# Longer wo runs and, in the last pass of a decode kernel's backward, held stores, a later dQ and an earlier ask for weight slabs

## The chip, the cores and the metric

The kernel runs on one core of one Trainium2 chip. The metric is device time of the whole program in microseconds (us), as the median of a kernel's runs. The kernel before took 2029.06 us (median of 3 runs, 2028.84 to 2034.46). Kernels are compared by their ratios to the kernel before.

"Half clock" below means stretches where the profile shows TensorE's granted clock at 0.50. The records of the clock hold 0.5 and 1.0 only; a 0.8 in a table is a mean over a stretch.

## The reference

Two layers of attention over a cache and of a feed-forward block with squared ReLU, for one token, then the gradients of everything by `jax.vjp`. Biases, reshapes and the set-up of inputs are cut.

```python
# D=1024, 32 query heads, 4 kv heads, 65536 cached positions, head size 128, F=3584, bf16
def attn(x, k_cache, v_cache, wq, wo):
    q = (x @ wq).reshape(1, 1, 32, 128).transpose(0, 2, 1, 3)
    k = jnp.repeat(k_cache, 8, axis=1); v = jnp.repeat(v_cache, 8, axis=1)
    p = softmax(jnp.einsum("bhqd,bhkd->bhqk", q, k) * 128 ** -0.5)
    o = jnp.einsum("bhqk,bhkd->bhqd", p, v)
    return o.transpose(0, 2, 1, 3).reshape(1, 1, 4096) @ wo
def ffn(x, w1, b1, w2, b2):
    h = x @ w1 + b1
    r = jnp.where(h > 0, h, 0)
    return (r * r) @ w2 + b2
x = x + attn(layernorm(x), k_cache, v_cache, wq, wo); x = x + ffn(layernorm(x), ...)
x = x + attn(layernorm(x), k_cache, v_cache, wq, wo); x = x + ffn(layernorm(x), ...)   # same weights
# outputs: x, and the gradients of x, k_cache, v_cache, wq, wo, w1, b1, w2, b2
```

Both layers use the same caches and weights, so dK and dV (67 MB each) are sums over two layers and are written once. The same holds for the weight gradients, which are sums of two outer products.

## The kernel before

The caches are read once for the forward of each layer and once or twice in the backward: four attention passes. The last pass reads V and K and writes dV and dK. In it, background work (the weight gradients, and products with the rows of wo and wq for the gradient that runs back through the layer) is taken up between the items of the pipeline. An item is 8 blocks of 128 positions of one kv head; the pass has 256 items, 64 per head ("group").

All big transfers use an arena of 1 MB places: 12, and eight more while the pass runs on, as the planes that hold the saved scores are given back group by group. SP (SyncE) issues the loads in order, POOL (GpSimd) the stores in order. A place whose store was just issued counts as five steps younger, and in the last pass a load takes the youngest place that has been free for nine steps.

```python
    def take_one(fill, load=False):
        by_age = sorted((t, i) for i, t in FREE.items())
        if load and PS["pass4"]:
            early = [i for t, i in by_age if t <= NOW["step"] - AHEAD]       # AHEAD = 9
            i = early[-1] if early else by_age[0][1]
            ...
    class Slot:
        def free(self, stored=False):
            for k in range(self.n):
                give_slot(self.i + k, STORE_STEPS if stored else 0)          # STORE_STEPS = 5

    def wo_slabs(g, ahead=1):                       # rows of 2 KB, one per partition and k
        v = rows_of(A_wo)
        return slabs("s_wo", lambda k, kn: v[:, g * R + k:g * R + k + kn, :], R, 4, 1024, ahead, True)

    def g_rowdots(slab_it, nk, vcol, nj, finish, name):
        ...
        for kc, slab in slab_it:
            if vbc is None:
                vbc = yield from g_bcast_vec(vcol, nj)
            elif kc % 4 == 0:
                for _ in range(WAIT_STEPS):         # 5 items between one slab and the next
                    yield "wait"
            t = mvs.tile([P, n], BF, name="mv_t", tag="mv_t", bufs=2)
            nc.vector.tensor_tensor(out=t[:, :], in0=slab, in1=vbc[:, :], op=ALU.mult)
            ...

        def by_group(self, p, gen):
            ...
                self.later.append((k * n + n // 2 if PS["pass4"] else k * n + n // 4, gen(g), g))
```

The last pass itself. `ps_gg` is the PSUM tile in which dV, dK and the weight gradients arrive; `evac` copies it to the arena on ACT (ScalarE) or DVE (VectorE), whichever has less planned work.

```python
        def outer16(name, out, key, xt, gg, j1):           # 16 blocks of dV or dK
            if j1 == 0:
                state[key] = Slot(name, True)
            stg = state[key].t[:, :].rearrange("p (j d) -> p j d", d=DH)
            for m in range(2):
                pg = ps_gg()
                for h in range(2):
                    nc.tensor.matmul(pg[:, 512 * h:512 * h + 512], lhsT=xt[64 * h:64 * h + 64, j1 // 8 + m, :],
                                     rhs=gg[64 * h:64 * h + 64, :, :].rearrange("p a b -> p (a b)"), ...)
                evac(stg[:, jj:jj + 8, :].rearrange("p j d -> p (j d)"), pg[:, :], kind="f32")
            if j1 + 16 == J:                               # J = 32
                nc.gpsimd.dma_start(out=out, in_=stg)      # 1 MB
                state.pop(key).free(stored=True)

        def k8(g, c8):                                     # dQ, and dK
            kb8 = kv8("k", g, c8)
            ...
            for i in range(8):
                nc.tensor.matmul(ps_dq[:, 0:w, :]..., lhsT=kb8[:, i, :], rhs=X[:, s:s + w, :]..., ...)
            ...
                if glast[g] // SU == su:
                    on_group(g)
            if 2 * j0 >= J:
                outer16("gstk", half(GKv, g, b), "stk", xt, state[("GG", g, su)][0], 2 * j0 - J)

        pipeline(items, [(vT, 0), (vS, TLEAD), (dV8, DV_LAG), (k8, B4_LAG)], bg, end)   # lags 0, 2, 3, 7

    def rank2(out, lhs, rhs):                              # weight gradients: 2 rows, one per layer
        n = out.shape[1]
        pg = ps_gg()
        for h in range(n // 512):
            r = slice(64 * h, 64 * h + 2)
            nc.tensor.matmul(pg[:, 512 * h:512 * h + 512], lhsT=lhs(r), rhs=rhs(r), ...)
        evac(out, pg[:, 0:n], kind="f32")

    def on4(g):                                            # when dQ of a group is complete
        if g != lastg[3]:
            bg.add(g_dn(L1, dn1, g, g == firstg[3]))       # product with the wq slabs
            bg.normal.append(gwq(g))
        else:
            PRE["rows"].run()
            ...
    attn_bwd4(3, L1, L3, on4, bg, b4, [(12 + B4_LAG, last_v), (12, pre_load("wq4", ...)), (5, fill4)])
    bg.drain()
    run(gwq(lastg[3]))                                     # the last wq gradient, from nothing
```

## Time and profile before

| | kernel before |
|---|---|
| median of the runs | 2029.06 us |
| span of the profiled execution | 2027.6 us |
| bytes moved, mean rate | 794.98 MB, 392 GB/s |
| last pass starts (first `xin` copy) | 1234.9 us |
| from there to item 252 of 256 | 743.4 us |
| item 252 to the last dq column, to the end | 24.9 us, 24.5 us |

Two views of waits over the last pass, 1235 us to the end: the DMA queue of SP, and the engines (total us, number, longest).

```profile
SPq L330 <- DMA out_dram<-arena: 537.2, 93, 13.4
```

```profile
PE ps_tr L1226 <- DMA arena<-in_A_v_cache_dram: 34.4, 10, 6.9
...
PE ps_acc L1306 <- DMA arena<-in_A_k_cache_dram: 24.8, 5, 9.5
```

SP waits for stores most of the time (537 of 793 us at this line alone). The windows view of the end, cut at the last dq column (2003.1) and the last eviction (2019.4); columns are stretch, length, busy time and count of PE, PEld, DVE, ACT and POOL, granted clock, DMA share, GB/s:

```profile
1978.20:2003.10 24.90, 23.30 (x322) 15.42 (x319) 18.35 (x26) 18.10 (x20) 4.03 (x7) 1.00 0.91 349
2003.10:2019.40 16.30, 9.94 (x109) 4.41 (x108) 9.78 (x25) 7.60 (x10) 1.78 (x3) 0.72 0.33 131
2019.40:2027.60 8.20, 0.00 (x0) 0.00 (x0) 0.00 (x0) 0.00 (x0) 0.73 (x1) 0.50 0.33 128
```

After the last eviction 1.05 MB remains to be stored (summed from the trace's packets): one place, 8.2 us.

### The profile page before, as it was taken

What the parts mean: (1) busy time and instruction counts of PE and PEld (TensorE: products, weight loads), DVE (VectorE), ACT (ScalarE), POOL (GpSimd) and SP (SyncE); (2) the same over time, 40 slices, a digit from 0 to 9 for tenths busy, and PEclk for the clock granted to TensorE, in tenths of its full rate; (3) what the DMA queues carried; (4) which work ended last, traced back from release to release, by engine and by line L of the source; (5) the groups of instructions that cost most, each with busy time, mean ns of one, the idle gap of its engine ahead of it and who ended that gap; (6) DMA issues with size and microseconds to landing.
All of it is one profiled execution on the core that took longest, in us unless ns stands there. A gap on an engine that the chain in (4) does not pass through costs nothing. (4 is left out here: it accounts for less than half of the span.)

```text
span 2027.6 us, 67015 instructions
## 1 busy us (share of the span) xinstructions
PE 1626.9 (80%) x30210; PEld 1332.9 (66%) x30210; DVE 1174.3 (58%) x2358; ACT 1044.6 (52%) x1613; POOL 144.5 (7%) x332
## 2 busy tenths in 40 slices
PE   6877888687877877787787887788788888698896
PEld 6877777687777776786676885455455555355554
DVE  5645455245554543544454457677667777577675
ACT  3434344144344352435363445587667667577675
POOL 0000000000000000000000001112121111111111
PEclk9989899799999987898998989889888889798888
DMA  9999999989999997899999977999999999999996
GB/s 389 420 420 420 419 423 397 371 362 420 420 418 420 420 399 279 352 420 421 420 417 412 401 267 266 370 410 423 422 420 421 393 423 396 363 402 423 421 379 245
DMA packets 110846, 794.98 MB, mean 392 GB/s; under 512 B 9425, under 2 KB 9439, under 8 KB 49375
## 3 DMA queue, kind: packets, MB, share of 16 engines
q1 hardware_dynamic: 86510, 624.99, 75.7%
q0 software_dynamic: 24048, 165.70, 19.8%
q8 instruction: 236, 3.87, 0.8%
q14 instruction: 52, 0.42, 0.1%
HBM read 624.96 MB, written 165.69 MB: 390 GB/s over the span
## 5 line engine op out<-in xcount | busy, mean ns | idle before, releaser
L153 DVE COPY kt<-ps_tr 128x1024 bf16<-128x1024 bf16 x724 | 497.8, 689 | 473.8 <-PE ps_tr L913 256.7
L150 ACT CAST arena<-ps_gg 128x1024 bf16<-128x1024 f32 x452 | 439.9, 1009 | 219.0 <-PE ps_gg L1280 160.7
L913 PE MATMUL ps_tr<-ident_b,arena 128*128 128x128 bf16 x3840 | 310.2, 226 | 60.4 <-DMA arena<-in_A_k_cache_dram 45.1
L913 PEld LDWEIGHTS <-arena 128*128 128x128 bf16 x3840 | 234.0, 101 | 66.6 <-DMA arena<-in_A_k_cache_dram 48.1
L153 DVE CAST arena<-ps_gg 128x1024 bf16<-128x1024 f32 (+1 forms) x191 | 228.9, 1198 | 82.4 <-PE ps_gg L1280 48.0
L150 ACT COPY kt<-ps_tr 128x1024 bf16<-128x1024 bf16 x164 | 172.2, 1054 | 183.9 <-PE ps_tr L1105 126.0
L1280 PE MATMUL ps_gg<-GG,xt 64*128 64x512 bf16 x1024 | 211.6, 413 | 46.4 <-DVE arena L153 26.8
L1015 PE MATMUL ps_acc<-arena 128*128 128x64 bf16 (+4 forms) x4096 | 206.0, 196 | 45.7 <-DMA arena<-in_A_v_cache_dram 31.7
L1226 PE MATMUL ps_tr<-ident_b,arena 128*128 128x128 bf16 x1824 | 175.9, 234 | 35.3 <-DMA arena<-in_A_v_cache_dram 34.4
L931 PE MATMUL ps_sc<-L_qpad,kt 128*128 128x64 bf16 (+7 forms) x3584 | 183.4, 194 | 17.9 <-issue 11.5
L996 ACT ACTIVATE arena<-S_sb,L_negm 128x128 bf16<-128x128 f32 x256 | 165.4, 1002 | 57.8 <-DVE L_negm L981 57.7
L1105 PE MATMUL ps_tr<-ident_b,arena 128*128 128x128 bf16 x1920 | 156.3, 228 | 48.3 <-DMA arena<-in_A_v_cache_dram 48.3
L1015 PEld LDWEIGHTS <-arena 128*128 128x128 bf16 x4096 | 159.8, 100 | 50.0 <-DMA arena<-in_A_v_cache_dram 34.8
L1226 PEld LDWEIGHTS <-arena 128*128 128x128 bf16 x1824 | 119.5, 104 | 88.8 <-issue 49.6
L931 PEld LDWEIGHTS <-kt 128*128 128x128 bf16 x3584 | 153.3, 100 | 23.6 <-issue 14.6
L1105 PEld LDWEIGHTS <-arena 128*128 128x128 bf16 x1920 | 118.6, 102 | 52.2 <-DMA arena<-in_A_v_cache_dram 51.0
L1306 PE MATMUL ps_acc<-X,arena 128*128 128x64 bf16 (+3 forms) x2048 | 119.7, 199 | 24.8 <-DMA arena<-in_A_k_cache_dram 24.8
L996 ACT ACTIVATION_READ_ACCUMULATOR arena<-S_sb,L_negm 128x1 f32 x256 | 127.8, 499 | 0.0
L1306 PEld LDWEIGHTS <-arena 128*128 128x128 bf16 x2048 | 87.1, 102 | 59.9 <-issue 33.1
L1150 PE MATMUL ps_acc<-dsT,arena 128*128 128x64 bf16 (+7 forms) x2048 | 103.7, 195 | 20.0 <-DMA arena<-in_A_k_cache_dram 15.8
L1280 PEld LDWEIGHTS <-xt 64*128 64x128 bf16 x1024 | 61.3, 94 | 86.3 <-issue 46.8
L1259 PE MATMUL ps_sc<-DOB,kt 128*128 128x64 bf16 (+3 forms) x1824 | 117.5, 200 | 0.0
(266 smaller groups left out, 2169.3 us busy)
## 6 DMA issues: line engine op xcount, KB each, us to landing
arena<-in_A_k_cache_dram SPq DMA_DIRECT2D x86, 2048.0 KB, 21.5
arena<-in_A_v_cache_dram SPq DMA_DIRECT2D x83, 2048.0 KB, 21.4
out_dram<-arena POOLq DMA_DIRECT2D x151, 1024.0 KB, 11.4
arena<-in_A_v_cache_dram SPq DMA_DIRECT2D x76, 1024.0 KB, 16.5
arena<-in_A_k_cache_dram SPq DMA_DIRECT2D x76, 1024.0 KB, 16.8
arena<-in_B_w_dram SPq DMA_DIRECT2D x32, 896.0 KB, 5.8
arena<-in_A_wq_dram SPq DMA_DIRECT2D x22, 1024.0 KB, 13.8
arena<-in_A_wo_dram SPq DMA_DIRECT2D x18, 1024.0 KB, 17.5
```

What stands on the lines that cost most here:

```text
L150: nc.scalar.copy(out=out, in_=in_)
L153: nc.vector.tensor_copy(out=out, in_=in_)
L913: nc.tensor.transpose(pt[:, i, :], kb8[:, i, :], ident_b[:, :])
L931: nc.tensor.matmul(state["ps_s"][:, s:s + w, :].rearrange("p a b -> p (a b)"), lhsT=kt[:, i, :], rhs=L["qpad"][:, g, 0:w, :].rearrange("p ...
L996: nc.scalar.activation(out=E(p, g, c0, SU)[:, :, h], in_=S[:, h, :], func=ACTF.Exp, bias=L["negm"][:, g, su, h:h + 1], scale=SCALE, accum_ ...
L1015: nc.tensor.matmul(ps_o[:, 0:w, :], lhsT=vb8[:, i, :], rhs=E(p, g, c, w), start=(c % SU == 0), stop=(c % SU == SU - 1), skip_group_check=True)
L1105: nc.tensor.transpose(pt[:, i, :], vb8[:, i, :], ident_b[:, :])
L1150: nc.tensor.matmul(ps_dq[:, 0:w, :].rearrange("p a b -> p (a b)"), lhsT=kb8[:, i, :], rhs=dsT[:, s:s + w, :].rearrange("p a b -> p (a b)") ...
L1226: nc.tensor.transpose(pt[:, i, :], vb8[:, i, :], ident_b[:, :])
L1259: nc.tensor.matmul(state["ps_dp"][:, s:s + w, :].rearrange("p a b -> p (a b)"), lhsT=vt[:, i, :], rhs=DOB[:, g, 0:w, :].rearrange("p a b - ...
L1280: nc.tensor.matmul(pg[:, 512 * h:512 * h + 512], lhsT=xt[64 * h:64 * h + 64, j1 // 8 + m, :], rhs=gg[64 * h:64 * h + 64, :, :].rearrange(" ...
L1306: nc.tensor.matmul(ps_dq[:, 0:w, :].rearrange("p a b -> p (a b)"), lhsT=kb8[:, i, :], rhs=X[:, s:s + w, :].rearrange("p a b -> p (a b)"), ...
```

## The change

It has five intents, all but the first for the last pass. (1) wo is read in runs of 8 or 16 KB where rows of 2 KB were read; a small matmul with a constant matrix puts the vector in the order of the runs. (2) The slabs of wo and wq are asked for two at a time, 12 items ahead of their use, so that VectorE does not stand in front of one. (3) Stores are held back, one more every half or quarter group, up to six in the last group, so that loads go first; they are let go in the last iterations. A held store is issued after the newest eviction, not after its own data alone. (4) dQ runs four items behind dK. (5) The last wq gradient is prepared ahead, its stores are 512 KB, and the background is drained ten iterations before the end. A few small buffers change too. Cut to its core:

```diff
+    WAIT4 = 12
-    B4_LAG = TLEAD + J // 8 + 1
+    DK_LAG = TLEAD + J // 8 + 1
+    B4_LAG = DK_LAG + J // 8
+    def wo_runs(g, ahead=1):
+        v = A_wo[g * 1024:(g + 1) * 1024, :].rearrange("(p k) n -> p k n", k=8)
+        return slabs("s_wo", lambda k, kn: v[:, k:k + kn, :], R, 4, 1024, ahead, True)
+    def slabs_first(pair):
+        g = prefetch(pair)
+        for _ in range(WAIT4):
+            yield "wait"
+        return g
-            elif kc % 4 == 0:
+            elif kc % 4 == 0 and wait:
-                self.later.append((k * n + n // 2 if PS["pass4"] else k * n + n // 4, gen(g), g))
+                self.later.append((k * n + (4 if PS["pass4"] and k else n // 4), gen(g), g))
... (g_wo and g_dO: the order of the runs, by to_runs and from_runs)
+        it = (yield from slabs_first(wo_runs(g, 2))) if PS["pass4"] else wo_runs(g)[0]
+        yield from g_rowdots(it, R, dx[:], DC, fin, "%s_dO%d" % (L["name"], g), not PS["pass4"])
... (g_dn: the same with wq_slabs(g, 2))
+        def store(ins):
+            out, stg, sl = pend.popleft()
+            st = nc.gpsimd.dma_start(out=out, in_=stg)
+            tc.add_manual_dep(st.ins, ins.ins.name, ..., reason="stores follow the loads of later blocks")
+            sl.free(stored=True)
+        def held(g, c8):
+            k, i = divmod(place[(g, c8)], n_g)
+            n = 2 * k - (4 * i < n_g) - (2 * i < n_g) if k else 0
+            return min(n, state.get("cap", 2 * G))
+        def cap(n): ...                 # sets the cap to n, stores what is over it
-                nc.gpsimd.dma_start(out=out, in_=stg)
-                state.pop(key).free(stored=True)
+                pend.append((out, stg, state.pop(key)))
+                while len(pend) > held(g, c8):
+                    store(state["evac"])
-        pipeline(items, [(vT, 0), (vS, TLEAD), (dV8, DV_LAG), (k8, B4_LAG)], bg, end)
+        pipeline(items, [(vT, 0), (vS, TLEAD), (dV8, DV_LAG), (dK8, DK_LAG), (k8, B4_LAG)], bg,
+                 list(end) + [(2 + n, cap(n)) for n in range(6)])
+    def g_outer_last(...): ...          # row sets made ahead, stores of 512 KB
... (fill4 drains the background and prepares g_outer_last; on4 runs it)
-    attn_bwd4(..., [(12 + B4_LAG, last_v), (12, pre_load("wq4", ...)), (5, fill4)])
-    bg.drain()
-    run(gwq(lastg[3]))
+    attn_bwd4(..., [(12 + B4_LAG, last_v), (24, pre_load("wq4", ...)), (10, fill4)])
```

## The prediction

> **What bounds the kernel now.** I read the page first, part 2, which cuts the span into 40 slices of 50.7 us.
>
> ```profile
> DMA  9999999989999997899999977999999999999996
> GB/s 389 420 420 420 419 423 397 371 362 420 420 418 420 420 399 279 352 420 421 420 417 412 401 267 266 370 410 423 422 420 421 393 423 396 363 402 423 421 379 245
> ```
>
> The DMA engines are the bound: the page counts 794.98 MB, and where nothing disturbs the flow they move 420 to 424 GB/s. At 423 GB/s all bytes would take 1879 us; the span is 2027.6 us. So 148 us are holes, and a change of order can only win holes. I take the lost time of a stretch as its length x (1 - rate/423). The share of busy DMA engines misleads here: it reads 9 where the rate is down to 370, so I go by GB/s.
>
> The change is mostly in the last pass (dK and dV stored while K and V are read), which starts at about 1235 us. The windows view of that pass (stretch, length, busy time and count per engine, granted clock, DMA share, GB/s):
>
> ```profile
> 1240.00:1260.00 20.00, 18.41 (x259) 10.78 (x259) 16.43 (x33) 14.55 (x15) 4.08 (x8) 1.00 0.53 186
> 1260.00:1340.00 80.00, 59.48 (x715) 36.34 (x716) 46.80 (x73) 44.79 (x53) 12.65 (x25) 0.81 0.99 383
> 1340.00:1580.00 240.00, 199.19 (x2532) 126.93 (x2529) 175.87 (x311) 169.30 (x205) 42.39 (x79) 0.89 1.01 421
> 1720.00:1740.00 20.00, 4.92 (x76) 3.40 (x75) 4.48 (x6) 4.86 (x7) 1.07 (x2) 0.67 1.02 422
> 1740.00:1760.00 20.00, 16.71 (x162) 10.19 (x162) 13.78 (x25) 13.90 (x19) 2.83 (x5) 0.64 0.75 285
> 1760.00:1820.00 60.00, 54.86 (x737) 34.31 (x735) 47.79 (x79) 43.47 (x47) 12.29 (x24) 0.97 1.01 402
> 1960.00:1985.50 25.50, 24.77 (x340) 15.83 (x337) 21.69 (x38) 20.90 (x24) 5.26 (x9) 1.00 0.94 338
> 1985.50:2003.30 17.80, 16.32 (x222) 10.92 (x221) 12.91 (x21) 12.63 (x14) 2.88 (x5) 1.00 0.86 354
> 2003.30:2027.60 24.30, 9.94 (x109) 4.41 (x108) 9.61 (x24) 7.40 (x10) 2.51 (x4) 0.64 0.34 131
> ```
>
> Lost: 11.2 and 7.6 us at the start of the pass, 6.5 and 3.0 us at 1740 to 1820, then 5.1, 2.9 and 16.8 us from 1960 on; the stretches not shown (1580 to 1620 at 384 GB/s, 1660 to 1720 at 400, 1920 to 1960 at 401) lose 3.7, 3.3 and 2.1 us. From 1260 on that is 51 us.
>
> The waits and the chain that ended last name the hole near 1740:
>
> ```profile
> DVE mv_t L549 <- DMA arena<-in_A_wo_dram: 16.5, 1, 16.5
> PE ps_gg L1280 <- DVE arena L153: 17.3, 1, 17.3
> 1711.14 10.81 DMA out_dram<-arena
> 1722.45 18.47 DMA arena<-in_A_wo_dram
> ```
>
> A store lands, its place is given to a slab of wo, the slab takes 18.5 us behind a full queue, and VectorE, which runs in order, stands 16.5 us in front of it with all evictions behind it. While it stands, DMA still runs at 422; afterwards nothing is queued and the rate drops to 285.
>
> The end: the trace's packets show the last load landing at 1985.6 us, and 9.64 MB of stores starting after 1985. Those need 22.8 us at 423 GB/s and get 42. The last dq column (`L_dqT`) is written at 2003.3; the chain from there:
>
> ```profile
> 2003.86 2.10 PE ps_acc L656 x64
> 2007.71 0.70 DVE rowb L153
> 2010.50 1.02 ACT arena L150
> 2018.17 1.24 DVE arena L153
> ```
>
> So 24.3 us follow the last dq, with 3.15 MB to store in them.
>
> **What the Trainium skill says.** "DMA: Bandwidth & Descriptors", section Issuing engines are not separate DMA queues: transfers started by SyncE and by GpSimd run on the same 16 engines and interleave. The trace agrees: SP's loads and POOL's stores together make the 421 GB/s of 1340 to 1580, no more than loads alone (420). Holding a store back therefore makes no bandwidth; it only decides who goes first. The same page, Anatomy of one DMA, says that DMA engines do not wait on semaphores, the issuing sequencer does. That fits the 537.2 us, in 93 waits, that SP's load line (L330) spends on landing stores: the next load stands behind a place not yet free. "Perfetto Trace Analysis", DMA Optimizations, says that longer pieces use memory better and names 2 KB to 4 or 8 KB. Here a 2 KB packet has a median of 85 ns, an 8 KB one 309 ns, a 16 KB one 614 ns: 385, 424 and 427 GB/s on 16 engines. So the penalty of 2 KB is some 10%, not a multiple.
>
> **The change, part by part.**
>
> *wo in long runs.* Of the 32 MiB of wo read, three groups of 2 MiB in each of four passes change: 25.2 MB, 12,288 packets of 2 KB. A packet of 85 ns becomes 614/8 = 77 ns or 309/4 = 77 ns per 2 KB: 8 ns x 12,288 / 16 = 6.2 us, three quarters of it in the first three attention passes, which run at the DMA's rate. Price: per group one matmul with 64 columns (0.2 to 0.4 us by the small matmuls of this page) and five small VectorE operations of 0.15 to 0.3 us, 12 times, on engines with room (VectorE 58% busy). **-6.2 us.**
>
> *Slabs asked for 12 items ahead.* The pass takes (1978 - 1260)/236 = 3.04 us per item (times of the `xin` copies for items 16 and 252), so 12 items are 36 us, against the 18.5 us of the slab and about 30 us for the slowest wo slab. The wait of 16.5 us should go. It is worth what DMA lost, not 16.5: 6.5 us, and half of the 3.0 us of catching up. **-8 us.** wq slabs get the same lead; no wait of theirs is prominent in the list.
>
> *Stores held back.* One more store is kept each quarter or half group, up to 6 in the last group; they use the places that the E planes give back after each group. (Counting the kernel's own allocations: free places when a load picks one were 14 to 17 in the last group before, and are 8 to 10 now, while the age of the place picked stays 9 to 14 steps.) 6 MiB in hand mean loads up to 6.29 MB / 423 = 14.9 us earlier, provided that compute follows. It has some room: PE is busy 83% in 1340 to 1580, but 97% in 1960 to 1985, where PE, not DMA, is the limit. I count two thirds. **-10 us**, seen as stores that fill the weak rate after 1960.
>
> *dQ four items after dK, wq gradient prepared.* The last dK stores start before the last dQ matmuls, which only moves work. After dq, the built order on PE now has dq's rows, eight outer products and no second row set; the two row sets of the other factor are made earlier, background is drained ten steps before the end, and the last stores are 512 KB instead of 1 MB. Before: last eviction 16.1 us after dq, end 8.2 us later. After: rows about 3 us, eight outer products on two evicting engines some 8 us, last store and end about 5. **24.3 to 16: -8 us.**
>
> *At the start* dK's K block is first touched four items later, but the places are still full of kept V blocks, so one K load fewer is in before the pass (an estimate from the allocations), and two wo slabs now sit for 20 items in 12 places. **+2 us.** The new constants and the 7 KB row through the arena cost well under 1 us.
>
> Sum: -6.2 - 8 - 10 - 8 + 2 = -30, from 2029 to **1999 us**.
>
> **Rivals.** (a) *Places bind instead.* Held stores and early slabs use the places, SP waits longer on stores and loads trickle as at 1260 to 1340 (383 GB/s). For: group 0 has 12 places only and the slabs now take two for 60 us. Against: 1340 to 1580 ran full with 9 to 11 free places. If it holds, the middle gains nothing and the time is about 2012 to 2020. (b) *PE binds the end.* PE is 97% busy from 1960; if compute cannot run ahead, the held stores only wait for the end and are written after it: head start nil, 2008 or so. (c) *Everything works.* From 1260 on 302.7 MB at 423 GB/s take 716 us; with the start's 7.6 us and 5 us for the end, less 6.2 us for wo, it ends near 1982. That is the floor, 2.3% below.
>
> **Range and chances.** 2% faster is 1988.5, which needs nearly all of (c), so I give it 15%. Slower by 2% (2070) would need a new stall larger than any in this pass: 4%. The rest is within 2%. Eight times in ten: 1985 to 2017.
>
> **What would show it.** Right: 8 KB or 16 KB packets on wo and some 12,000 fewer 2 KB packets; no wait of VectorE on wo over 5 us and no slice near 363 in the middle; over 400 GB/s in the last 40 us but for the final 10; dq to end about 16 us. Wrong: SP waiting on stores much more than 537 us with rates of 380 to 400 in the middle groups; PE at 97% for more than the last 60 us; the last stores queued well after the last eviction, which would mean too many were held.

## More of the kernel before

The lines of the page that the argument comes back to: busy time per engine, the granted clock in 40 slices of the span (tenths of full speed), and the packets by size.

```profile
PE 1626.9 (80%) x30210; PEld 1332.9 (66%) x30210; DVE 1174.3 (58%) x2358; ACT 1044.6 (52%) x1613; POOL 144.5 (7%) x332
...
PEclk9989899799999987898998989889888889798888
...
DMA packets 110846, 794.98 MB, mean 392 GB/s; under 512 B 9425, under 2 KB 9439, under 8 KB 49375
```

No engine is busy over 80% of the time, but PE is the next in line after DMA, and its clock is at half speed for some 390 us of the span, so nine tenths of full speed in the mean.

## The result, and the profile after

The changed kernel took 2046.74 us (median of 4 runs, 2041.71 to 2050.36), the kernel before 2028.95 (4 runs, 2028.04 to 2034.46). The ratio is 1.008, with a 95% interval of 1.0051 to 1.011: slower by some 18 us, within 2%, and outside the predicted range. A ratio here is the mean time of one kernel's runs over that of the other's of the same rounds, so not quite the ratio of the medians that are quoted. All outputs are right.

The page after; the same lines, and the rates of the 40 slices (51.2 us each):

```profile
PE 1657.7 (81%) x30228; PEld 1344.0 (66%) x30228; DVE 1177.9 (57%) x2405; ACT 1046.5 (51%) x1613; POOL 145.3 (7%) x334
...
PEclk9999999799999997989998998888879897876986
...
GB/s 392 419 425 420 425 424 398 379 340 421 425 419 425 424 376 316 362 421 425 419 421 409 386 249 286 377 393 422 408 353 385 425 423 334 375 421 365 380 344 314
DMA packets 101038, 794.98 MB, mean 388 GB/s; under 512 B 9473, under 2 KB 9487, under 8 KB 37135
```

The same bytes moved in 9,808 fewer packets, and the early slices are as good or better. PE has the same work but for 18 matmuls (30228 against 30210), and is busy 30.8 us longer: that is clock, not work. In the clock line the last twelve slices hold one 7 before, and three 7s and two 6s after; the rate dips (353, 334, 365, 344) stand in the same part.

The windows of the last pass, some of those of the prediction again (`...` marks where others are left out), with the end cut at the last dq column (2011.9) and the last eviction (2030.7):

```profile
1340.00:1580.00 240.00, 208.80 (x2572) 129.38 (x2571) 171.09 (x308) 163.48 (x191) 41.46 (x76) 0.84 0.96 390
...
1720.00:1740.00 20.00, 19.14 (x169) 10.56 (x168) 11.53 (x17) 11.06 (x12) 2.84 (x5) 0.57 0.89 328
...
1960.00:1990.00 30.00, 23.17 (x272) 13.65 (x272) 16.64 (x28) 15.15 (x16) 4.22 (x7) 0.74 0.81 299
...
2011.90:2030.70 18.80, 13.29 (x118) 5.93 (x111) 11.80 (x25) 9.85 (x12) 7.38 (x13) 0.62 0.83 327
2030.70:2048.50 17.80, 0.00 (x0) 0.00 (x0) 0.01 (x1) 0.00 (x0) 1.04 (x2) 0.50 0.77 304
```

Three things to see. The long middle stretch, 1340 to 1580, which ran at 421 GB/s before, runs at 390. That is not yet lost time: by the `xin` copies the changed kernel does 80.2 items in it and the kernel before 78.8, but with 3.0 MB of stores and 4.6 MB of loads fewer, which are still to come. From 1720 to 1740 VectorE no longer stands (DVE busy 11.53 against 4.48), but PE is now busy 19.14 of 20 us at a clock of 0.57, with 169 matmuls. And the end has 17.8 us in which nothing is computed and 5.41 MB are stored.

The waits over the last pass, SP's queue first, then the engines:

```profile
SPq L345 <- DMA out_dram<-arena: 595.6, 92, 20.7
```

```profile
PE ps_tr L1288 <- DMA arena<-in_A_v_cache_dram: 45.0, 11, 10.4
...
PE ps_acc L1399 <- DMA arena<-in_A_k_cache_dram: 31.8, 11, 9.9
...
DVE mv_t L576 <- ACT vbc L547: 0.7, 1, 0.7
```

VectorE's wait for wo is gone. SP's loads wait 58 us more for stores, and PE waits 76.8 us for V and K where it waited 59.2.

Where the 20.9 us between the two profiled spans come from can be read off the times of the `xin` copies, one per four items, and of the last dq column. Relative to before: the pass starts 5.7 us earlier, and the first three groups (items 0 to 192) take 563 us against 572. Then the last group to item 252 takes 198 us against 172 (+26.1 before rounding), item 252 to dq takes 21.9 against 24.9, and dq to the end 36.6 against 24.5. The gain of 14 us up to item 192 is there in these two executions; the last group and the tail lose it and 21 us more.

How a stretch becomes bad is best seen near 1525. Windows of 5 us, then the issues of POOL and of SP around it (start, length, engine, what; in brackets the idle time before and what ended it):

```profile
1515.00:1520.00 5.00, 4.50 (x33) 2.33 (x34) 1.96 (x3) 1.93 (x2) 0.00 (x0) 0.50 1.01 428
1520.00:1525.00 5.00, 5.00 (x46) 2.75 (x46) 3.07 (x5) 3.04 (x3) 0.00 (x0) 0.50 0.62 259
1525.00:1530.00 5.00, 5.00 (x38) 2.49 (x36) 1.68 (x3) 3.04 (x3) 0.00 (x0) 0.50 0.00 0
1530.00:1535.00 5.00, 5.00 (x43) 2.77 (x41) 3.41 (x5) 2.34 (x3) 2.22 (x4) 0.50 0.68 270
1535.00:1540.00 5.00, 4.06 (x77) 2.79 (x76) 3.55 (x10) 2.87 (x4) 0.00 (x0) 0.99 1.03 351
```

```profile
1512.39 0.53 POOL L1341 DMA_DIRECT2D out_dram<-arena  x1 [0.27 <-ACT arena L162]
1530.60 1.07 POOL L1341 DMA_DIRECT2D out_dram<-arena  x2 [17.67 <-DVE arena L164]
```

```profile
1516.05 0.33 SPq L345 DMA_DIRECT2D arena<-in_A_k_cache_dram  x1
1534.88 0.33 SPq L345 DMA_DIRECT2D arena<-in_A_v_cache_dram  x1
```

PE is busy without a break at half clock and does some 40 matmuls in 5 us where it does 77 at full clock. POOL waits 17.7 us for the eviction that its next store is tied to (line 1341 is the store of a held place). SP can issue no load from 1516 to 1535, because the place it wants is that store's: the store lands at 1534.82 and the load is issued at 1534.88. The DMA engines run dry: 0 GB/s for 5 us. So here a compute engine that was off the critical path puts itself on it, through stores and places, once its clock has halved. Holding is not needed for such a wait: in no_hold POOL waits 15.8 us for an eviction between 1515 and 1545. In the whole last pass of the profiled executions PE stood at half clock for 197 us before and 287 after; outside the last pass the two differ by 4 us.

### The profile page after: what moved, and what is told of

The parts are those of the page before. It is cut to its first block, busy times and chain, and to the rows that moved or that the text cites.

```text
span 2048.5 us, 67031 instructions
## 1 busy us (share of the span) xinstructions
PE 1657.7 (81%) x30228; PEld 1344.0 (66%) x30228; DVE 1177.9 (57%) x2405; ACT 1046.5 (51%) x1613; POOL 145.3 (7%) x334
## 5 line engine op out<-in xcount | busy, mean ns | idle before, releaser
L162 ACT CAST arena<-ps_gg 128x1024 bf16<-128x1024 f32 (+1 forms) x451 | 441.8, 1010 | 247.4 <-PE ps_gg L1367 204.1
L975 PE MATMUL ps_tr<-ident_b,arena 128*128 128x128 bf16 x3840 | 308.2, 225 | 40.5 <-DMA arena<-in_A_k_cache_dram 27.0
L1367 PE MATMUL ps_gg<-GG,xt 64*128 64x512 bf16 x1024 | 222.2, 434 | 26.2 <-ACT arena L162 11.7
L1288 PE MATMUL ps_tr<-ident_b,arena 128*128 128x128 bf16 x1824 | 183.0, 240 | 46.9 <-DMA arena<-in_A_v_cache_dram 45.0
L1167 PE MATMUL ps_tr<-ident_b,arena 128*128 128x128 bf16 x1920 | 158.4, 229 | 43.0 <-DMA arena<-in_A_v_cache_dram 41.0
L993 PEld LDWEIGHTS <-kt 128*128 128x128 bf16 x3584 | 153.0, 100 | 17.9 <-issue 9.2
L1399 PE MATMUL ps_acc<-X,arena 128*128 128x64 bf16 (+3 forms) x2048 | 112.2, 202 | 32.0 <-DMA arena<-in_A_k_cache_dram 31.8
L1321 PEld LDWEIGHTS <-kt 128*128 128x128 bf16 x1824 | 87.9, 104 | 46.5 <-issue 45.2
## 6 DMA issues: line engine op xcount, KB each, us to landing
arena<-in_A_k_cache_dram SPq DMA_DIRECT2D x86, 2048.0 KB, 21.1
arena<-in_A_k_cache_dram SPq DMA_DIRECT2D x76, 1024.0 KB, 10.4
arena<-in_A_wo_dram SPq DMA_DIRECT2D x22, 1024.0 KB, 12.8
arena<-in_A_wq_dram SPq DMA_DIRECT2D x20, 1024.0 KB, 13.1
```

The costliest lines, as they stand in the source:

```text
L162: return nc.scalar.copy(out=out, in_=in_)
L975: nc.tensor.transpose(pt[:, i, :], kb8[:, i, :], ident_b[:, :])
L993: nc.tensor.matmul(state["ps_s"][:, s:s + w, :].rearrange("p a b -> p (a b)"), lhsT=kt[:, i, :], rhs=L["qpad"][:, g, 0:w, :].rearrange("p ...
L1167: nc.tensor.transpose(pt[:, i, :], vb8[:, i, :], ident_b[:, :])
L1288: nc.tensor.transpose(pt[:, i, :], vb8[:, i, :], ident_b[:, :])
L1321: nc.tensor.matmul(state["ps_dp"][:, s:s + w, :].rearrange("p a b -> p (a b)"), lhsT=vt[:, i, :], rhs=DOB[:, g, 0:w, :].rearrange("p a b - ...
```

## The experiments

Each experiment is one edit of the changed kernel unless its text says otherwise. `before` is the median of the runs of the kernel before. The table has what the traces say of each (us; one profiled execution each, which lies up to 8.5 us off the median, as in runs_only with 2025.3 against 2033.9, so differences of a few us in these columns show little): the start of the last pass, from there to item 192, from 192 to 252, to the last dq column, to the end, and the half-clock time between start and item 252.

| kernel | median | before | ratio (95%) | start | to 192 | to 252 | to dq | to end | half clock |
|---|---|---|---|---|---|---|---|---|---|
| before | 2028.95 | | | 1234.9 | 572 | 172 | 24.9 | 24.5 | 177 |
| after | 2046.74 | 2028.95 | 1.0080 (1.0051 to 1.0110) | 1229.2 | 563 | 198 | 21.9 | 36.6 | 253 |
| after_pad | 2036.92 | 2031.10 | 1.0038 (1.0006 to 1.0070) | 1226.6 | 561 | 190 | 23.7 | 34.9 | 164 |
| before_pad | 2030.11 | 2031.10 | 1.0006 (0.9971 to 1.0042) | 1233.8 | 572 | 173 | 24.9 | 24.6 | 143 |
| no_hold | 2040.01 | 2031.10 | 1.0053 (1.0023 to 1.0083) | 1229.2 | 577 | 182 | 33.1 | 21.4 | 217 |
| no_lead | 2034.51 | 2031.10 | 1.0020 (0.9993 to 1.0048) | 1228.3 | 549 | 192 | 29.5 | 34.0 | 195 |
| dq_with_dk | 2054.05 | 2029.35 | 1.0114 (1.0084 to 1.0143) | 1228.0 | 564 | 191 | 30.4 | 34.6 | 218 |
| no_lead_no_hold | 2029.80 | 2029.35 | 1.0005 (0.9970 to 1.0041) | 1226.4 | 575 | 172 | 30.3 | 20.9 | 205 |
| prep_and_runs | 2031.67 | 2029.35 | 1.0009 (0.9981 to 1.0037) | 1225.5 | 573 | 174 | 31.8 | 25.8 | 206 |
| runs_only | 2033.85 | 2029.35 | 1.0011 (0.9976 to 1.0047) | 1224.4 | 573 | 172 | 26.8 | 27.3 | 212 |
| runs_first3 | 2026.92 | 2031.45 | 0.9982 (0.9965 to 1.0000) | 1228.2 | 570 | 175 | 25.8 | 23.2 | 181 |
| no_lead_free_early | 2031.74 | 2031.45 | 1.0005 (0.9985 to 1.0024) | 1229.8 | 551 | 193 | 30.8 | 25.9 | 191 |
| lead_apart | 2047.53 | 2031.45 | 1.0083 (1.0052 to 1.0114) | 1228.4 | 548 | 199 | 31.3 | 33.9 | 188 |
| lead_spaced | 2042.14 | 2031.45 | 1.0046 (1.0012 to 1.0081) | 1229.0 | 556 | 200 | 21.5 | 36.9 | 242 |
| lead_late | 2054.68 | 2029.47 | 1.0122 (1.0098 to 1.0146) | 1229.3 | 569 | 206 | 22.1 | 33.9 | 229 |
| lead_wo_only | 2029.50 | 2029.47 | 1.0002 (0.9983 to 1.0020) | 1224.9 | 540 | 200 | 24.6 | 37.7 | 198 |
| first3_one_early | 2029.72 | 2029.47 | 1.0006 (0.9990 to 1.0021) | 1223.5 | 570 | 188 | 20.8 | 22.7 | 191 |
| free_early_pad | 2024.91 | 2029.47 | 0.9977 (0.9960 to 0.9994) | 1228.1 | 551 | 193 | 30.0 | 27.1 | 184 |
| wq_one_place | 2038.55 | 2030.20 | 1.0039 (1.0028 to 1.0049) | 1227.5 | 560 | 191 | 24.8 | 33.3 | 236 |
| wo_early_free_pad | 2026.25 | 2030.20 | 0.9977 (0.9965 to 0.9989) | 1229.2 | 548 | 200 | 21.1 | 30.3 | 181 |

The theory after reading the two traces: the early slabs and the held stores take places; loads come later; PE idles, drops to half clock, and at half clock is slower than DMA; the outer products of two rows may keep it there. The rivals: the places alone; the stores after the end alone; the later dQ.

### after_pad, before_pad: the weight gradients with 64 rows, 62 of them zero

```diff
-            r = slice(64 * h, 64 * h + 2)
+            r = slice(64 * h, 64 * h + 64)
... (the row tiles get all 128 partitions and are set to zero once)
```

> The changed kernel, with the rank-2 outer products given 64 contraction rows in place of 2, the other 62 zero: the same columns, the same results, some 35 short memsets more. Theory C (clock): in the last pass the granted clock falls to half after a wait of PE, and stays there because the work at half clock, weighted by its rows, stays under some 0.75 of a window; the 2-row products count for nothing in it. Half-clock time in the last pass was 197 us before and 287 us after. C expects it to fall under 200 us here, no cold spell of 58 us, and 2047 us to fall to 2000 to 2025. Theory H (the held stores take the loads' places and chain loads to later evictions) expects no change: 2040 to 2050 us, with the holes at the same height.

> The kernel before with the same padding. Theory C: half-clock time in the last pass falls from 197 us to 150 us or less, and the time by 5 to 15 us, to 2014 to 2024; the wait for the wo slab stays. If rows do not count for the clock, 2027 to 2034 us, as before.

The products give the same numbers and take the same number of columns. In the changed kernel padding took the half-clock time before item 252 from 253 to 164 us, the longest cold spell before the tail from 58.0 to 17.1 us, and the time from 2046.74 to 2036.92, between the ranges of the two theories. The two ratios come from different calls and their intervals overlap. In the kernel before padding took half-clock time from 177 to 143 us and the time did not move. The single runs bear the clock out, and not only the profiled ones: their mean granted clock is 0.884 to 0.896 after and 0.905 to 0.912 with padding, and for the kernel before 0.893 to 0.904 and 0.908 to 0.911 (four to seven runs each). The clock line of the page with padding:

```profile
PEclk9999999699999998889888997889889889888986
```

Of the last twelve slices none is under 8 now but the very last. So the rows that a matmul uses, not only its being busy, matter for when the clock comes back, and half clock was worth something like 10 us of the changed kernel's time and nothing that these runs can show before. It is not the whole loss.

### no_hold: the stores not held

```diff
-            return min(n, state.get("cap", 2 * G))
+            return 0
```

> The changed kernel with every store sent at once (none held), all else kept. Theory H: the loss goes, 2010 to 2030 us, with the middle of the last pass back over 415 GB/s and a longer weak end. Theory C: holding is not the cause, half-clock time stays near 250 us or more, and the time stays at 2035 to 2055 us.

2040.01, ratio 1.0053 against 1.0080 of the full change, with intervals that overlap. The middle of the pass (1340 to 1580) stays at 398 GB/s, so theory H, which expected over 415 GB/s and 2010 to 2030 us, does not hold. The tail fell from 36.6 to 21.4 us, since 0.98 MB and not 5.41 MB are left after the last eviction. The way to item 192 became longer by 14 us.

### no_lead: the slabs one at a time, in the middle of the group, as before

```diff
-        it = (yield from slabs_first(wo_runs(g, 2))) if PS["pass4"] else wo_runs(g)[0]
-        yield from g_rowdots(it, ..., not PS["pass4"])
+        yield from g_rowdots(wo_runs(g)[0], ...)
... (g_dn likewise with wq_slabs(g)[0]; by_group starts at k * n + n // 2 again)
```

> The changed kernel with the weight slabs asked for as before (one at a time, at half of a group, with the five waiting steps), all else kept. A third theory, L: the two slabs kept for 22 items and the row products in one burst make the new holes; then 2010 to 2030 us. C and H expect 2035 to 2055 us, with a wait on a wo slab of up to 16 us back.

2034.51, ratio 1.0020: the early lead costs 0.6%, some 12 us, in place of the gain of 8 that the prediction gave it. And the wait that it was to remove is back, at a wq slab now, in the waits of the last pass:

```profile
DVE mv_t L576 <- DMA arena<-in_A_wq_dram: 16.9, 1, 16.9
```

A stand of 16.9 us of VectorE is there, and the kernel is faster than the one without it.

### dq_with_dk: dQ in the same step as dK

```diff
-    B4_LAG = DK_LAG + J // 8
+    B4_LAG = DK_LAG
```

> The changed kernel with dQ in the same item as dK again (K blocks used 7 items after their V block, not 11), all else kept. In the changed kernel K loads are issued 3.5 items after the V position and used at 11, so 7.5 items ahead; in the kernel before 8.7. If the shift of dQ costs the lead (theory D), K's lead grows to 8 or more and the time falls to 2025 to 2038; if it does not matter, 2041 to 2050 us.

2054.05, ratio 1.0114: slower than the full change. So the later dQ is not what costs; inside the full change it may help, by about 7 us, but the intervals overlap. This rival falls.

### no_lead_no_hold, prep_and_runs, runs_only: the change taken apart further

The first has both edits above. The second has dQ with dK as well. The third also has the end of before, and so only the long wo runs are left.

```diff
 prep_and_runs, on top of no_lead and no_hold:
-    B4_LAG = DK_LAG + J // 8
+    B4_LAG = DK_LAG
 runs_only, on top of prep_and_runs:
-    attn_bwd4(..., [..., (24, pre_load("wq4", ...)), (10, fill4)])
+    attn_bwd4(..., [..., (12, pre_load("wq4", ...)), (5, fill4)])
+    bg.drain()
+    run(gwq(lastg[3]))
... (g_outer_last not used)
```

> The changed kernel with neither stores held nor slabs asked for early; wo in long runs, dQ four items late and the prepared end are left. Alone, taking the lead away gave 2034.5 and taking the holding away 2040.0, against 2046.7. If the two costs add up, 2046.7 - 12 - 7 = 2028 us; if they are one cost (early slabs and held stores both take the places from the loads), 2033 to 2040; if holding helps once the lead is gone, over 2035.

> As no_lead_no_hold, with dQ beside dK again: only wo in long runs and the prepared end are left of the change. From the first passes the runs give 5.7 us and the prepared end gave 3 us in no_hold (dq to end 21.4 us, before 24.5), so 2029 - 9 = 2020 us, 2014 to 2026, if these two parts are sound and all harm is in the others.

> Only wo in long runs is left (and small buffer changes). The last pass then starts 6 us earlier than in the kernel before and runs as before, with the wait on a wo slab: 2023 us, 2018 to 2028.

1.0005, 1.0009 and 1.0011: all the same as before, and as each other. So lead and holding together make the whole loss, and the rest of the change, predicted to win 12 us (-6.2 - 8 + 2), wins nothing that these runs can show. In the traces the start of the pass is 8.5 to 10.5 us earlier, more than the 4.7 us that the prediction gave the long runs there. The tail is 27.3 us without the prepared end, 25.8 with it, and 20.9 with the later dQ too, but item 252 to dq grows from 26.8 to about 31.

No_lead against no_lead_no_hold shows what holding does, without any slab in it: to item 192 it is 26 us ahead, the last group gives 20 back, and the tail is 13.1 us longer.

### runs_first3: the long runs in the first three passes only

```diff
+        if PS["pass4"]:
+            yield from g_rowdots(wo_slabs(g)[0], R, dx[:], DC, dO_finish(L, g), ...)
+            return
... (on top of runs_only)
```

> Only wo in long runs, and those in the first three attention passes alone; the last pass reads wo as before. Where long runs everywhere brought the last pass forward by 8 to 10 us in the profiles and the total not at all (2033.9 against 2029.4), this tells whether the last pass's own long runs (their extra matmul and row step) lose it again: then 2020 to 2025 us. If the total is 2028 to 2035 again, an earlier start of the last pass is not worth its length, whatever the form of wo.

2026.92, ratio 0.9982 (to 1.0000): about 4 us better, what the prediction gave to the first three passes (4.7). Against runs_only the medians say that long runs cost 7 us in the last pass, but the intervals overlap, and this stays inconclusive.

### no_lead_free_early: the held stores let go earlier

```diff
-                 list(end) + [(2 + n, cap(n)) for n in range(6)])
+                 list(end) + [(7 + 2 * n, cap(n)) for n in range(6)])
... (on top of no_lead)
```

> The changed kernel without the early slabs, with the held stores let go from 17 to 7 iterations before the end of the pipeline, not from 7 to 2. In no_lead 11.5 MB were stored after the last dq and 5.8 MB after the last eviction (18.8 us), while DMA ran at 307 GB/s between item 252 and the last dq. If the stores are held too long (theory T), the time after the last eviction falls from 18.8 to 8 to 12 us and the total from 2034.5 to 2022 to 2028. If PE or the store queue bounds the end, stores only crowd out the last K loads: 2031 to 2038.

The window from the last eviction to the end, in no_lead and then here:

```profile
2013.90:2032.70 18.80, 0.00 (x0) 0.00 (x0) 0.00 (x0) 0.01 (x1) 1.43 (x2) 0.50 0.79 310
```

```profile
2020.20:2030.50 10.30, 0.00 (x0) 0.00 (x0) 0.00 (x0) 0.02 (x1) 0.76 (x2) 0.50 0.56 218
```

8.5 us less with nothing but stores, because 2.23 MB are left there and not 5.79. The time is 2031.74 against 2034.51; the last eviction came 6.3 us later, so most of it was paid ahead.

### lead_apart, lead_spaced, lead_late: three ways to ask for the slabs more gently

```diff
 lead_apart: the two slabs six items from each other
-        g = prefetch(pair)
-        for _ in range(WAIT4):
-            yield "wait"
+        g, fetches = pair
+        for f in fetches:
+            f()
+            for _ in range(WAIT4 // 2):
+                yield "wait"
 lead_spaced: five items again between the products with the one slab and with the other
-        yield from g_rowdots(it, ..., not PS["pass4"])
+        yield from g_rowdots(it, ...)
 lead_late: wo asked for 20 items into the group of 64, not four
-        ... (k * n + (4 if PS["pass4"] and k else n // 4), gen(g), g)
+        ... (k * n + (n // 2 - WAIT4 if PS["pass4"] else n // 4), gen(g), g)
```

> The changed kernel with the two slabs of a group asked for six items apart, each, in place of both at once. If the loss of the early slabs (12 us) is the burst of 2 MB in front of the K and V loads (theory B), the slow stretches at items 96 to 112 and 160 to 176 (337 and 325 GB/s) rise over 390 and the time falls to 2032 to 2040. If it is the places that they take or the row products in one go, 2043 to 2052.

> The changed kernel with early slabs, but with the five waiting steps before the second half of each set of row products put back. If the eight row products in one go (some 6 us of VectorE and 8 us of ScalarE on top of the evictions) hold up evictions and so stores (theory R), 2032 to 2040 us; the second slab then stays five items longer in its place, so if places are what counts, 2048 to 2056.

> The changed kernel, its wo slabs still asked for 12 items ahead in pairs, but so that the row products fall at half of a group, as in the kernel before, not at its start. If the loss of the lead is the crowding of wo and wq work into the first half of a group, where holding also steps up (theory G), the time falls from 2047 to 2033 to 2040 us; if it is the two places kept for some 22 items (theory P), 2043 to 2052.

2047.53, 2042.14 and 2054.68. Two slabs in one burst were not the cause: lead_apart is where the full change is. The eight row products in one go were at most a part (ratio 1.0046, with an interval that overlaps the full change's). And lead_late, in which wo's slabs no longer sit beside wq's at the start of the group, was the slowest of all.

### lead_wo_only: wq's slabs as before, wo's early

```diff
-        it = (yield from slabs_first(wq_slabs(g, 2))) if PS["pass4"] else wq_slabs(g)[0]
-        yield from g_rowdots(it, DC, L["dqT"][:, gsl(g)], ..., not PS["pass4"])
+        yield from g_rowdots(wq_slabs(g)[0], DC, L["dqT"][:, gsl(g)], ...)
```

> The changed kernel with wq read as before (one slab at a time, asked for when needed) and only wo early. If the early wq slabs carry the loss (they follow the wo slabs, at items 97 to 122 of the pass, where DMA falls to 337 GB/s), 2034 to 2040 us; if the wo slabs do, 2043 to 2050; in equal parts, 2040.

2029.50: taking back the lead of one of the two weights takes 17 us off the changed kernel. Its rates over the 40 slices (50.7 us each):

```profile
GB/s 392 421 424 421 423 424 397 373 355 421 425 420 424 425 404 286 359 422 424 421 419 415 397 290 266 369 423 412 415 402 360 424 399 403 383 421 386 411 354 283
```

The slices that fell to 353 and 334 in the changed kernel read 402 and 403 (the one after the first reads 360, not 385). So it is the early wq slabs that cost; wo's alone, on top of no_lead, are a gain of about 4 us if anything (1.0002 against 1.0020, with intervals that overlap). The end is still weak (354, 283).

### wq_one_place: wq's slabs early, but one at a time

```diff
-        it = (yield from slabs_first(wq_slabs(g, 2))) if PS["pass4"] else wq_slabs(g)[0]
-        yield from g_rowdots(it, DC, ..., not PS["pass4"])
+        it = (yield from slabs_first(wq_slabs(g, 1))) if PS["pass4"] else wq_slabs(g)[0]
+        yield from g_rowdots(it, DC, ...)
```

> The changed kernel with the wq slabs still asked for 12 items early, but one at a time, so that they keep one place, not two; wo as in the changed kernel. If the two places kept for some 22 items are the loss (theory P), the time comes near that of lead_wo_only, 2028 to 2037 us; if it is wq's early work as such, in whatever place, 2041 to 2052.

2038.55 in 20 runs, ratio 1.0039 (1.0028 to 1.0049): between lead_wo_only (1.0002) and the full change (1.0080). About half of the loss goes with the second place and the row products in one go, and half stays with one early slab.

### first3_one_early: before's slabs, each asked for some items earlier

```diff
+            it = prefetch(wo_slabs(g, 1))
+            for _ in range(7):
+                yield "wait"
-            yield from g_rowdots(wo_slabs(g)[0], ..., dO_finish(L, g), ...)
+            yield from g_rowdots(it, ..., dO_finish(L, g), ..., 10)        # 10 items before the second slab, not 5
... (on top of runs_first3; by_group starts seven items earlier)
```

> runs_first3 (2026.9 us) with the wo slabs of the last pass asked for earlier, one at a time: 7 items more for the first and 5 more for the second. The wait of VectorE on a wo slab (16.5 us, 9.5 us of lost DMA time with the catching up) should go: 2017 to 2022 us. If the place kept longer costs as in the changed kernel, 2027 to 2033.

2029.72, ratio 1.0006: nothing gained over runs_first3 (0.9982, with intervals that overlap). But the run does not do what it was meant to. The waits of VectorE in its last pass:

```profile
DVE X L1333 <- DMA arena<-in_A_wo_dram: 13.5, 1, 13.5
```

VectorE still stands, 13.5 us where it stood 18.0 in runs_first3, at the same item (171) and until the same wo slab lands, now in front of another of its instructions: in the trace SP issues that slab at item 168.6, in the kernel before at 168.5. The edit asks earlier in the program, but the slab is not issued earlier. What it is worth to fill the hole that the prediction started from, where nothing is held, stays open.

### free_early_pad, wo_early_free_pad: what a better version would have

The first is no_lead_free_early with padded products. The second is lead_wo_only with padded products and the earlier letting go.

```diff
 both:
+ rank-2 products of 64 rows, as in after_pad
+                 list(end) + [(7 + 2 * n, cap(n)) for n in range(6)])
 free_early_pad: slabs as in no_lead; wo_early_free_pad: slabs as in lead_wo_only
```

> no_lead_free_early (2031.7 us) with the rank-2 products padded to 64 rows, which gave the changed kernel 10 us and the kernel before nothing. Theory C: with stores held, the last pass depends on PE's clock, so half-clock time to item 252 falls from 191 us to under 150 and the time to 2020 to 2027. If the gain seen in after_pad was another effect of order, 2028 to 2036.

> lead_wo_only (2029.5 us) with the held stores let go from 17 to 7 iterations before the end (worth 3 us in no_lead, and 8 us after the last eviction) and the rank-2 products padded to 64 rows (worth 7 us on top of that): 2029.5 - 3 - 7 = 2019 us if the three gains add, 2013 to 2026; against the kernel before at 2029 to 2031. Time after the last eviction 10 to 13 us, not 19.4; half-clock time to item 252 under 185 us.

2024.91 (6 runs) and 2026.25 (22 runs of it and 43 of before; 2019.0 to 2034.9). Both ratios are 0.9977. The first lies in the range that was expected; the second just above it, so the three gains do not add up to 2019. The half-clock time of free_early_pad was to fall under 150 us and reads 184, but its profiled execution was the slowest of six: the mean clock of its runs is 0.904 to 0.915, against 0.895 to 0.903 in no_lead_free_early. The second is the surer, 0.9965 to 0.9989: 0.23% below the kernel before, and, from the two ratios, 1.0% below the changed one. It beats both, by less than the 2% that would be called faster.

## Why the prediction was wrong, step by step

The place of the 2% band was right (0.81 on "within 2%"), the sign was not: the sum of -30 us came out as +18. The step that failed was the second term, and the third with it; of the fourth the runs show little.

**wo in long runs (-6.2).** Right in its packets and in the first three passes. "Under 8 KB" less "under 2 KB" went from 39,936 to 27,648 packets, a drop of exactly the 12,288 counted; the pass starts 5 to 11 us earlier in every variant that has them; runs_first3 gains 0.18%. (The median landing of a 1 MB slab fell from 17.5 to 12.8 us in the change, but that is not the runs: without the early ask it is 18.0 in no_lead and 20.2 in no_lead_no_hold.) The last quarter, in the last pass, was not seen: runs_only as a whole stands at 1.0011.

**Slabs asked for 12 items ahead (-8).** This step failed, in its price. The wait went, as predicted, and the time did not go with it: the lead cost 12 us (no_lead). Against the 8 us the prediction set no more than a part of the 2 us at the start. The sentence "no wait of theirs is prominent", which gave wq the lead for free, hid the cost: of the lead, wo's half does no harm, and wq's makes the loss (lead_wo_only, 17 us). Whether 6.5 us of weak DMA at 1740 to 1760 *belong* to VectorE's stand, as the prediction has it, is not settled: no_lead and no_lead_no_hold have stands of 16.9 and 14.4 us and are faster than the full change, so a stand does not decide the time, but the run that was to remove it alone (first3_one_early) did not remove it.

Why the wq slabs cost that much is not shown. They are asked for when a group's dq is complete, and the two stay through 12 items of waiting. wq_one_place says that the second place, with the products in one go, is about half of it. But the count of places does not explain it: added up in the traces from issue to last use, the six wo and six wq slabs of the first three groups keep places for 364 items in the changed kernel and for 369 in the kernel before, where SP issues them far ahead too. Among kernels that hold stores the sum goes with the time in part (179 in no_lead, 276 in lead_wo_only, 295 in wq_one_place), but lead_late, slower than all of these, has 324.

Nor does the lead of the loads explain it: the V loads of the whole pass are issued 6.5 items ahead of their use in the changed kernel, 7.2 in lead_wo_only and in no_lead, 7.7 before; but wq_one_place has 7.3, and no_hold has 8.6, the longest of these, and its PE waits 90.7 us for V and K, more than the 76.8 of the full change. In lead_late the wo slabs of the second group are issued (items 94 and 96) only while the wq slabs are being read (92 to 97), and it is slower still. What is left stays open.

Rival (a), places, was named with a time of 2012 to 2020, 13 to 21 us over the predicted 1999; its signs came true (SP waits 595.6 us, the middle groups at 390 GB/s), but the result is 48 us over. The rate is a weak sign, as said: no_lead has 396 GB/s there, and reaches item 192 in 549 us.

**Stores held (-10).** The condition written into this term, "provided that compute follows", is where it fell. The pass did run ahead, more than the 14.9 us counted: 26 us at item 192 (no_lead against no_lead_no_hold, one execution each). At item 252, 6 us were left of it. The stores then had to be written when nothing was left to do beside them: 5.4 to 5.8 MB after the last eviction (1.05 before), 17.8 to 18.8 us. The prediction's own sign for "too many were held" was this line. In all, holding costs 3 us of the median in the pair without the lead (1.0020 against 1.0005) and 5 with it (1.0080 against 1.0053); each pair has overlapping intervals, so neither shows it alone. Letting go earlier mends the tail, and part of the time. Rival (b), PE binds the end, told this story, but as "head start nil, 2008".

**dQ late, last gradient prepared (-8).** The work after dq got shorter at most a little. Without holding, dq to the end fell from 24.5 to 20.9 or 21.4 us, not to 16, and item 252 to dq grew by 5 us or more, which eats it. Kernels without the prepared end scatter from 22.7 to 27.3 us, and prep_and_runs, which has it, reads 25.8. In the full change this gain is not to be seen, since the held stores fill the tail (36.6 us).

**What was missing.** The prediction took PE's 83% in the middle as room, and read its clock of 0.89 as a fact of the kernel. The room vanishes when the clock halves. At 3.04 us per item DMA sets the pace; from 1837 to 1882 in the changed kernel, nearly all at half clock, 12 items take 44.6 us, or 3.7 us each. The longest spell is 58 us, 17 periods of 3.41; before, the longest was 27.3 us, which began while PE stood for the late wo slab. The windows view of it, and PE's groups by shape (line, operation, output and inputs, rows by columns, count, busy us, mean ns, idle before and its cause):

```profile
1822.00:1880.00 58.00, 50.38 (x398) 26.89 (x398) 24.33 (x35) 27.55 (x29) 7.11 (x14) 0.50 0.98 374
```

```profile
L1367 PE MATMUL ps_gg<-GG,xt 64*128 64x512 bf16 x54 | 16.7, 599 | 0.2 <-DVE arena L164 0.2
L1288 PE MATMUL ps_tr<-ident_b,arena 128*128 128x128 bf16 x96 | 14.2, 308 | 10.4 <-DMA arena<-in_A_v_cache_dram 10.4
...
L1437 PE MATMUL ps_gg<-arena,rowa 2*128 2x512 bf16 x19 | 6.7, 603 | 0.0
```

PE waits 10.4 us for V, until 1829.4. Then it is busy without a break, 50.4 us to 1880, and stays at 0.50 all the same. A good part of its work uses 64 of the 128 rows (54 products of 512 columns) or two (19 products).

The Trainium skill, "TensorE: Matmul & The Clock Gate", section Part 1: The HAM clock gate (the "warmup" mystery), says that the clock is half when idle and full after at least one busy window of about 3.4 us, and that the window runs free. The steps of 3.41 us and the two values agree with the trace. "Busy", as this profile counts it (the ends of matmuls are modelled), does not: in the 5 us windows from 1520 to 1535 PE is busy 5.00 of 5.00 us and stays at 0.50. I counted, for each 3.41 us at half clock in the last pass of the changed kernel, the columns of all matmuls, each weighted by rows used over 128. Windows after which the clock stayed low have a median of 2,700, those after which it rose 3,440; the 95th percentile of the first (3,070) and the 5th of the second (2,910) lie close together. In the kernel before these medians are 2,000 and 3,500, in after_pad 1,600 and 3,400, and in the long spell, after its wait, all groups of the view together make 42,500 such columns, 2,900 in each of the 14.8 periods.

That the rows count is shown by padding (253 to 164 us of half clock); the number of about 3,000 is a correlation, not a test. It carries over, though: a limit of 3,070 columns, between the two groups of the changed kernel, puts 33 of the 1,229 half-clock periods of the other 19 traces on the wrong side. (At half clock 128-column matmuls of 128 rows start 107 ns apart in this trace, so a period has room for some 4,080 such columns, and the limit is about three quarters of it, as theory C had it.) Over all 20 traces the best limit on the columns without weights misplaces 296 periods of 1,312, and the best limit on the busy share 352. The same page's section HAM oscillation — how this bites in real kernels tells of DMA waits that throttle PE again and again, at the cost of the cold work; the trace agrees, and adds that here the cold work in turn starves the DMA.

PE has as many idle gaps over 2.5 us in the last pass after (11, 64 us) as before (10, 68 us). So it is not more gaps but longer spells behind them. Padding gives about 10 us of the 18 back, in line with this; that the profiled executions of lead_apart and lead_wo_only have nearly the same half-clock time (188 and 198 us to item 252) and take 2042.6 and 2028.5 us says that the clock does not explain the wq slabs' part alone.

## What to carry to other kernels

A removed wait is worth at most what the bound engine loses by it, and the change that removes it has a price of its own, which a prediction has to name; here the part of the change that "has no prominent wait" had only the price. Look in the trace whether an edit did what it says before its time is read: a slab that is asked for earlier in the program need not be issued earlier. When an engine has 17% of room, ask what its clock would have to do to take the room away, and what of its work does not count toward getting the clock back. Work that is held back for a slack at the end must fit that slack: let it go while there is still compute to lie beside it.

## What the Trainium skill lacked or had wrong

- "TensorE: Matmul & The Clock Gate", table of the two states: a busy window does not suffice. PE was busy 15 us without a break at 0.50 (1520 to 1535), and 50.4 us in the longest spell; of 687 half-clock periods with PE busy over 99%, in the last passes of all 20 traces, 365 were followed by the full clock. Matmuls with 2 of 128 rows seem to count for next to nothing; with 64 rows, 62 of them zeros, half-clock time fell from 253 to 164 us. The page names no such dependence on rows.
- "Perfetto Trace Analysis", DMA Optimizations: it says that batching small transfers, "2KB → 4KB or 8KB", "can dramatically improve throughput", and does not tell transfers from the packets in them. Here the transfers of wo were 1 or 2 MB before and after and only the packets grew: 2 KB ones moved at 385 GB/s and 8 KB ones at 424 by their durations, and the time fell by 0.18% (runs_first3).
- None of the pages that I read has this ring: a slow PE delays an eviction, the eviction a store, the store a place, and the place the next load (17.7 us of POOL's wait, 0 GB/s from 1525 to 1530).
